# The last feed-forward block of an S4D layer with a ReLU network: its sums are turned back through five banks of PSUM instead of one

## The chip, the cores and the metric

The kernel runs on one core of one Trainium2 chip. The engines named here are TensorE (PE in the profile; PEld is its weight load), VectorE (DVE), ScalarE (ACT), GpSimd (POOL) and SyncE (SP). Matmul results go to PSUM, of which a core has eight banks of 128 x 512 fp32; VectorE and ScalarE read them from there. The metric is the time of one execution in microseconds, the median of several runs; less is better.

## What is computed

A block with adaptive layer norm: six vectors are made from a condition `c`, a normalised input goes through a long convolution (the S4D part, by Fourier transforms) and is added back, and the result goes through a feed-forward network with ReLU and is added back again. The second half is what the change is about:

```python
    h = _layernorm(x, axis=-1) * (1 + cb) + sb
    x = x + gb * _B_ref(h, B_w1, B_w2)
    ...
    def _B_ref(x, w1, w2):
        h = jnp.einsum("bsd,df->bsf", x, w1)
        zero = jnp.zeros_like(h)
        h = jnp.maximum(h, zero)
        return jnp.einsum("bsf,fd->bsd", h, w2)
```

There are 2048 tokens of 576 columns, and the hidden width is 4608. All values are fp32.

## The kernel before

The tokens are worked on in four blocks of 512 (`NB = 4`). The convolution of the first block is computed ahead; from then on the feed-forward network of block b runs on TensorE while the other engines prepare block b + 1.

**The feed-forward loop.** `ffn` (a generator, lines 1128 to 1276) goes over 4 x 36 steps, one for each 128 hidden columns of each block. A step makes 128 hidden columns for 512 tokens in one PSUM bank (tag `hps`, two banks, line 1179), ScalarE and VectorE take it out as a high and a low part (`hh`, `hl`, lines 1184 and 1185), and `second` multiplies both with the second weight and adds into five accumulators (`acc0` to `acc4`, five banks, line 1204). Each accumulator holds 128 of the 576 output columns, the last one the remaining 64 twice over (a high and a low part of the weights stacked), with the 512 tokens along the free dimension. With one more bank (tag `cps`, `nps = 1`) for transposes and all else, the eight banks are taken.

**The end of a block.** When the 36th step of a block has been added, `ffn` calls `evacuate` (line 1278): five ScalarE instructions (line 1283) copy the accumulators to SBUF, times the column's `gb`; the four full ones go to `oT` and the last to `o4`. `finish` (line 1289) then turns the result so that tokens lie on the partitions. For each of four groups of 128 tokens it makes four TensorE transposes into the `cps` bank (line 1301), adds the bank to the residual `x2` with VectorE (line 1304, 512 columns), makes one product with `ident2` (an identity stacked twice, which adds the two halves of the last accumulator) into the same bank (line 1307), adds that (line 1310, 64 columns), and stores 128 rows of 576 columns to DRAM from GpSimd's queue (line 1312). For blocks 0 to 2 `finish` is a generator whose pieces are worked in between the next block's matmuls; for block 3 nothing is left beside it, and `main` runs it through at the end (line 699).

**What sets the order.** Instructions are issued in the order of the code and wait for each other's results through semaphores that the framework puts in; each engine takes its own in order. A tile of a pool with one buffer can be written again only when its last reader is done. So with `nps = 1` the transposes of a token group wait until VectorE has read the `cps` bank.

Of the kernel before, what the change touches and what calls it, by code (L numbers as in the profile page):

```python
# [10 lines left out]
F32 = mybir.dt.float32  # L11
F32R = mybir.dt.float32r
I32 = mybir.dt.int32
AF = mybir.ActivationFunctionType
ALU = mybir.AluOpType
# [3 lines left out]
P = 128  # L19
L = 2048  # L20
D = 576
N = 128
F = 4608
NB = 4
NF = F // P
# [440 lines left out]
class Body:  # L466
# [187 lines left out]
    def main(self, ctx, kg, first, late):  # L654
        nc, tc, I = self.nc, self.tc, self.I
        sm = self.pool(ctx, "sm1")
        self.fcU, self.fcK, self.gc = (sm.tile([P, 4, 2, P], F32, name=n) for n in ("fcU", "fcK", "gc"))
        self.ended = -1
        self.gens = []
        self.start = self.ffn(self.gens)  # L660
        with ExitStack() as c:
            self.conv0(ctx, c, kg, first, late)
        self.nps = 1
        self.cps = self.pool(ctx, "cps", space=PSUM)
        self.fps = self.pool(ctx, "fps", space=PSUM)

        self.cvs = ExitStack()

        def pool(s):
            self.cv = self.pool(self.cvs, f"cv{s}")  # L670

        def block0():
            yield from kg.rest(
                self.cps,
                [(h + 6 * i, b) for h in range(6) for i, b in enumerate(((1, 2, 3), (1,)))],
            )
            self.xp.append(self.pool(ctx, "xb"))
            self.x2p.append(self.xp[1])
            pool(1)
            yield from self.conv(1)  # L680

        def block1():
            yield from self.finish(0)
            yield -1
            self.cvs.close()
            yield from kg.rest(self.cps, [(h, (2, 3)) for h in range(6, 12)])
            pool(2)
            yield from self.conv(2)

        def block2():  # L690
            yield from self.finish(1)
            yield from self.conv(3)

        self.gens += block0(), block1(), block2(), self.finish(2)
        with tc.issue_after(self.ends[0]), tc.issue_after(self.ends[1]):
            next(self.start)
        for _ in self.start:
            pass
        for _ in self.finish(3):
            pass  # L700
        self.cvs.close()

    def spec(self, name):
# [424 lines left out]
    def ffn(self, gens):  # L1128

        nc, I, ff = self.nc, self.I, self.ff  # L1130
        v = self.v
        n = NB * NF
# [3 lines left out]
        def load_r1(g):  # L1136
            r1[g] = ff.tile([P, 5, P], F32, tag="r1", bufs=2, name="r1")
            self.kept(nc.sync.dma_start(out=r1[g], in_=I["w1"][g % NF]))

        def load_r2(g):  # L1140
            r2[g] = ff.tile([P, D], F32, tag="r2", bufs=2, name="r2")
            self.kept(nc.sync.dma_start(out=r2[g], in_=I["w2"][(g % NF) * P : (g % NF) * P + P, :]))

        def low1(g):
            w = w1[g] = ff.tile([P, 2, 5, P], F32R, tag="w1", bufs=2, name="w1")
            if g >= NF:
                nc.sync.dma_start(
                    out=w[:, 1].rearrange("p k c -> p (k c)").bitcast(F32), in_=self.L1d[g % NF]
                )

        def split1(g):

            w, r = w1[g], r1.pop(g)
            nc.scalar.activation(w[:, 0], r, AF.Copy)  # L1154
            if g < NF:
                v(w[:, 1], r, w[:, 0], op=ALU.subtract)
                late.append((self.L1d[g], w[:, 1].rearrange("p k c -> p (k c)")))

        def split2(g):

            w = w2[g] = ff.tile([P, 1152], F32R, tag="w2", bufs=3, name="w2")
            r = r2.pop(g)
            nc.scalar.activation(w[:, 0:D], r, AF.Copy)  # L1163
            if g < NF:
                v(w[:, D:640], r[:, 512:D], w[:, 512:D], op=ALU.subtract)
                v(w[:, 640:], r[:, :512], w[:, :512], op=ALU.subtract)
                late.append((self.L2d[g], w[:, D:]))
            else:
                nc.sync.dma_start(out=w[:, D:].bitcast(F32), in_=self.L2d[g % NF])

        def first(g):
            xh, xl, xs = self.xT[g // NF]
            w = w1.pop(g)
            ps = self.fps.tile([P, 512], F32, tag="hps", bufs=2, name="hps")
            ops = [(w[:, 0, 4], xs), (w[:, 1, 4], xs)]
            for k in range(4):
                ops += [(w[:, 0, k], xh[:, k]), (w[:, 0, k], xl[:, k]), (w[:, 1, k], xh[:, k])]
            for i, (a, x) in enumerate(ops):
                nc.tensor.matmul(ps, a, x, start=(i == 0), stop=(i == 13))  # L1179
                if i == 6:  # L1180
                    step(g)
            hh = ff.tile([P, 512], F32R, tag="hh", bufs=3, name="hh")
            hl = ff.tile([P, 512], F32R, tag="hl", bufs=3, name="hl")
            nc.scalar.activation(hh, ps, AF.Relu)  # L1184
            nc.vector.scalar_tensor_tensor(hl, ps, 0.0, hh, op0=ALU.max, op1=ALU.subtract)  # L1185
            return hh, hl
# [27 lines left out]
        def step(g):  # L1214

            at[0] += 1
            at[1] = g
            target = self.rate(g // NF) * (at[0] % 144 or 144)
            gen = gens[g // NF]
            v = pe = 0.0  # L1220
            room = (9.0, 7.0, 7.0, 7.0)[g // NF] - sum(recent[-3:])
            recent.append(0.0)
            while done[0] < target and v < min(room, 2.7) and pe < 2:
                w = next(gen, 0)
                if gen.gi_frame is None or w == -1:
                    return
                if w is None:
                    pe += 1
                    done[0] += 0.7
                else:  # L1230
                    v += w
                    recent[-1] = v
                    done[0] += w
# [13 lines left out]
        for g in range(n + 2):  # L1247
            if g < n:
                if g + 2 < n:
                    load_r1(g + 2)  # L1250
                if g + 1 < n:
                    load_r2(g + 1)
                for dst, src in late:
                    nc.sync.dma_start(out=dst, in_=src.bitcast(F32))
                late.clear()
                if g:
                    split2(g)
                if g and g + 1 < n:
                    split1(g + 1)
                waiting.append((g, *first(g)))  # L1260
                if g + 2 < n:
                    low1(g + 2)
                step(g)
            if g > 1:
                e = waiting[0][0]
                second(*waiting.pop(0))
                if e % NF == NF - 1:
                    self.evacuate(e // NF)
            if g == 2:
                yield  # L1270
            if g < n:
                step(g)
                if g % NF == NF - 1:
                    for _ in gens[g // NF]:
                        pass
                    done[0] = 0.0

    def evacuate(self, b):
        o = self.spec("oT").rearrange("p a b c -> p (a b c)")[:, :2048]
        o = o.rearrange("p (i t) -> p i t", i=4)  # L1280
        o4 = self.cv.tile([P, 512], F32, tag="o4", bufs=1, name="o4")
        for i in range(5):
            self.nc.scalar.activation(
                o[:, i] if i < 4 else o4, self.acc[i], AF.Copy, scale=self.m["gb"][:, i : i + 1]
            )
        self.oT = (o, o4)
        self.ended = b

    def finish(self, b):

# [103 lines left out]
```

## Time and profile before

| what | before |
|---|---|
| median of 3 runs | 1411.89 us (1408.91 to 1412.83) |
| the profiled execution's own time | 1413.05 us |
| its span, first to last instruction | 1411.3 us |
| mean granted TensorE clock | 0.928 of full speed |
| last accumulating matmul of block 3 starts | 1396.33 us |
| last store issued | 1407.09 us |

The profile is of one execution. Its times are counted from the span's start, and 1.75 us of the execution's own time lie outside the span. Rows of the timeline name a line of the kernel; the line numbers are those of the code before, and after the change lines from 700 on are one less, from the new function on 33 more.

### The profile page before, as it was taken

Reading aid. Unit: us, or ns where it says so; the run is one execution under the profiler, and the core shown is the slowest. Engines: PE = TensorE matmul, PEld = TensorE weight load, DVE = VectorE, ACT = ScalarE, POOL = GpSimd, SP = SyncE. Lnnn points to the kernel's source line nnn. Section 1 sums busy time; section 2 is a strip of 40 time slices with the busy share of each in tenths; the row PEclk is TensorE's granted clock in tenths of the full one; section 3 lists DMA queues with packets and bytes.
Section 4 is the critical chain, followed back from the end, with each engine's and each line's share of the span. In section 5 each row is a group of like instructions: output and inputs, shape, how many; then the busy total and the mean of one; then the engine's idle time right before and its main releaser. Section 6 shows DMA issues by size and latency. Waiting matters only on the chain. (4 is left out here: it accounts for less than half of the span.)

```text
span 1411.3 us, 25953 instructions
## 1 busy us (share of the span) xinstructions
PE 1243.7 (88%) x10600; PEld 984.0 (70%) x10600; DVE 881.8 (62%) x1353; ACT 502.7 (36%) x1008; POOL 197.8 (14%) x271
## 2 busy tenths in 40 slices
PE   6023677999999988799999989999999999999997
PEld 3023455778777776577777867777887888888885
DVE  4987968999875796658744986263999232010111
ACT  6975224222223412432233224434322253233331
POOL 1776311011111100021011010000010000000000
PEclk9555688999999999899999999999999999999998
DMA  6665777689887947489678995665988657666661
GB/s 189 226 245 197 282 262 285 222 290 328 277 292 242 322 155 296 159 318 374 223 249 309 330 368 167 194 227 175 386 313 316 200 156 212 201 191 199 196 187 57
DMA packets 135510, 346.36 MB, mean 245 GB/s; under 512 B 23456, under 2 KB 23744, under 8 KB 135392
## 3 DMA queue, kind: packets, MB, share of 16 engines
q1 hardware_dynamic: 108112, 221.57, 48.2%
q0 software_dynamic: 26992, 122.55, 23.6%
q8 instruction: 83, 1.36, 0.4%
q10 hardware_dynamic: 288, 0.59, 0.1%
q14 instruction: 35, 0.29, 0.1%
HBM read 263.26 MB, written 81.40 MB: 244 GB/s over the span
## 5 line engine op out<-in xcount | busy, mean ns | idle before, releaser
L1204 PE MATMUL acc<-hh,w 128*128 128x512 f32 x1296 | 429.2, 404 | 6.0 <-DVE w L488 6.0
L1179 PE MATMUL hps<-xh,w 128*128 128x512 f32 x1152 | 398.1, 406 | 0.0
L1185 DVE SCALAR_TENSOR_TENSOR hl<-hps,hh 128x512 fp32r<-128x512 f32 x144 | 99.1, 688 | 323.6 <-ACT hh L1184 323.3
L1204 PEld LDWEIGHTS acc<-hh,w 128*128 128x128 f32 x1296 | 244.5, 190 | 59.8 <-DVE w L488 7.6
L1204 PE MATMUL acc<-hl,w 128*128 128x512 f32 x720 | 280.5, 399 | 0.0
L1179 PEld LDWEIGHTS hps<-xh,w 128*128 128x128 f32 x1152 | 219.3, 191 | 48.2 <-ACT xh L982 0.6
L1179 PE MATMUL hps<-xl,w 128*128 128x512 f32 x576 | 230.0, 399 | 0.2 <-DVE xl L987 0.2
L1184 ACT ACTIVATE hh<-hps 128x512 fp32r<-128x512 f32 x144 | 86.0, 598 | 338.8 <-PE hps L1179 336.1
L1163 ACT ACTIVATE w<-r 128x576 fp32r<-128x576 f32 x144 | 98.7, 686 | 259.6 <-PE acc L1204 217.3
L1204 PEld LDWEIGHTS acc<-hl,w 128*128 128x128 f32 x720 | 136.1, 189 | 28.5
L1179 PEld LDWEIGHTS hps<-xl,w 128*128 128x128 f32 x576 | 110.3, 191 | 24.8 <-DVE xl L987 1.3
L246 PE MATMUL kps<-W,W 128*32 128x16 f32 x2304 | 39.8, 219 | 92.9 <-POOL W L59 60.0
L1154 ACT ACTIVATE w<-r 128x640 fp32r<-128x640 f32 x144 | 105.5, 733 | 38.5 <-DMA L1d<-w 33.5
L1179 PE MATMUL hps<-xs,w 128*128 128x512 f32 x288 | 103.6, 421 | 11.0 <-ACT w L1154 4.4
L246 PEld LDWEIGHTS kps<-W,W 128*32 128x32 f32 x2304 | 37.6, 151 | 96.0 <-POOL W L59 61.4
L421 PEld LDWEIGHTS kps<-W1r,W2r 128*32 128x32 f32 x3456 | 68.5, 146 | 31.1 <-issue 21.7
L488 DVE TENSOR_TENSOR Y<-Y,T 128x1152 f32<-128x1152 f32 x64 | 85.0, 1351 | 0.2
L421 PE MATMUL kps<-W1r,W2r 128*32 128x48 f32 (+2 forms) x3456 | 77.2, 238 | 7.8 <-issue 4.9
L1312 POOL DMA_DIRECT2D out_dram<-x x16 | 8.8, 550 | 492.4 <-DVE x L1310 492.4
L1179 PEld LDWEIGHTS hps<-xs,w 128*128 128x128 f32 x288 | 54.2, 192 | 24.9 <-DVE w L488 5.3
L488 DVE TENSOR_TENSOR w<-r,w 128x64 fp32r<-128x64 f32 (+2 forms) x108 | 58.3, 572 | 14.3 <-ACT w L1154 12.0
L725 ACT ACTIVATE Z<-ps_f 128x288 f32<-128x288 f32 x104 | 42.2, 409 | 68.6 <-PE ps_f L724 62.5
(192 smaller groups left out, 1414.6 us busy)
## 6 DMA issues: line engine op xcount, KB each, us to landing
r<-in_w_dram SPq DMA_DIRECT2D x144, 320.0 KB, 3.7
r<-in_w_dram SPq DMA_DIRECT2D x144, 288.0 KB, 3.5
w<-L1d SPq DMA_DIRECT2D x108, 320.0 KB, 3.0
w<-L2d SPq DMA_DIRECT2D x108, 288.0 KB, 3.2
W2r<-W2d POOLq DMA_DIRECT2D x18, 1536.0 KB, 10.0
W2d<-W SPq DMA_DIRECT2D x12, 1536.0 KB, 7.7
Ua<-Ud POOLq DMA_DIRECT2D x15, 1152.0 KB, 10.7
W<-W1d POOLq DMA_DIRECT2D x18, 768.0 KB, 10.0
```

What stands on the lines that cost most here:

```text
L246: self.nc.tensor.matmul(ps[32 * dd : 32 * dd + 32, 12 * u + q, :], W2[:, r, :, ch], W1[:, u, :, r, ch], start=(r == 0), stop=(r == 1),)
L421: nc.tensor.matmul(ps[32 * dd : 32 * dd + 32, q, :], W2[:, r, :, ch], W1[:, :na, r, ch], start=(r == 0), stop=(r == 1),)
L488: return self.kept(self.nc.vector.tensor_tensor(*args, **kw))
L725: nc.scalar.activation(Z[:, n2, c], ps[:, :PC], AF.Copy)
L1154: nc.scalar.activation(w[:, 0], r, AF.Copy)
L1163: nc.scalar.activation(w[:, 0:D], r, AF.Copy)
L1179: nc.tensor.matmul(ps, a, x, start=(i == 0), stop=(i == 13))
L1184: nc.scalar.activation(hh, ps, AF.Relu)
L1185: nc.vector.scalar_tensor_tensor(hl, ps, 0.0, hh, op0=ALU.max, op1=ALU.subtract)
L1204: nc.tensor.matmul(acc[i], a, x, start=(f == 0 and j in (0, 3, 6, 9, 12)), stop=(f == NF - 1 and j in (2, 5, 8, 11, 13)),)
L1312: nc.gpsimd.dma_start(out=ov[:, n2], in_=x2[:, n2])
```

## The change

Block 3 no longer goes through `evacuate` and `finish(3)`, but through a new method, `last_block`, that `main` calls at the same place. Since the last hidden column has been multiplied by then, the two `hps` banks are free, and each accumulator's bank is free once it has been copied.

- The copies to SBUF alternate: ScalarE does accumulators 0, 2 and 4, VectorE 1 and 3.
- The transposes go accumulator by accumulator, each into the matching quarter of four banks: one bank for each token group, the two of `hps`, the `cps` bank and the bank of `acc0`.
- The four products for the last 64 columns go to a fifth bank, that of `acc1`, and one VectorE instruction adds them for all four token groups.
- The stores are issued from SyncE's queue.

```diff
@@
-        for _ in self.finish(3):
-            pass
+        self.last_block()
         self.cvs.close()
@@
-                if e % NF == NF - 1:
+                if e % NF == NF - 1 and e < n - 1:
                     self.evacuate(e // NF)
@@
+    def last_block(self):
+
+        nc, m = self.nc, self.m["gb"]
+        x2 = self.x2.pop(NB - 1)
+        ov = self.out[L - 512 :, :].rearrange("(m n) d -> m n d", n=4)
+        o = self.spec("oT").rearrange("p a b c -> p (a b c)")[:, :2048]
+        o = o.rearrange("p (i t) -> p i t", i=4)
+        o4 = self.cv.tile([P, 512], F32, tag="o4", bufs=1, name="o4")
+        tok = [slice(n2 * P, (n2 + 1) * P) for n2 in range(4)]
+        ps = []
+        for i in range(5):
+            t = o[:, i] if i < 4 else o4
+            if i % 2:
+                nc.vector.tensor_scalar(t, self.acc[i], m[:, i : i + 1], None, op0=ALU.mult)
+            else:
+                nc.scalar.activation(t, self.acc[i], AF.Copy, scale=m[:, i : i + 1])
+            if i == 0:
+                for tag, bufs in (("hps", 2), ("hps", 2), ("acc0", 1)):
+                    ps.append(self.fps.tile([P, 4, P], F32, tag=tag, bufs=bufs, name="ps_l"))
+                ps.insert(2, self.cps.tile([P, 4, P], F32, tag="cps", bufs=self.nps, name="ps_l"))
+            if i < 4:
+                for n2 in range(4):
+                    nc.tensor.transpose(ps[n2][:, i], o[:, i, tok[n2]], self.ident)
+        ps4 = self.fps.tile([P, 4, 64], F32, tag="acc1", name="ps_l4")
+        for n2 in range(4):
+            nc.tensor.matmul(ps4[:, n2], o4[:, tok[n2]], self.ident2, start=True, stop=True)
+        for n2 in range(4):
+            xo = x2[:, n2, 0:512]
+            nc.vector.tensor_tensor(xo, ps[n2].rearrange("p a b -> p (a b)"), xo, op=ALU.add)
+            if n2 == 0:
+                xo = x2[:, :, 512:D]
+                nc.vector.tensor_tensor(xo, ps4, xo, op=ALU.add)
+            nc.sync.dma_start(out=ov[:, n2], in_=x2[:, n2])
```

VectorE at the end of the program, before: `hl` is the low part of a hidden step, `x_3` the residual of block 3, `ps_o` the one bank with the transposes or with the last columns.

```order
L1185 SCALAR_TENSOR_TENSOR hl<-hps,hh 128x512 x31
L1304 TENSOR_TENSOR x_3_9308<-ps_o,x_3_9308 128x512
L1310 TENSOR_TENSOR x_3_9308<-ps_o_12827,x_3_9308 128x64
L1304 TENSOR_TENSOR x_3_9308<-ps_o,x_3_9308 128x512
L1310 TENSOR_TENSOR x_3_9308<-ps_o_12837,x_3_9308 128x64
L1304 TENSOR_TENSOR x_3_9308<-ps_o,x_3_9308 128x512
L1310 TENSOR_TENSOR x_3_9308<-ps_o_12847,x_3_9308 128x64
L1304 TENSOR_TENSOR x_3_9308<-ps_o,x_3_9308 128x512
L1310 TENSOR_TENSOR x_3_9308<-ps_o_12857,x_3_9308 128x64
```

The same engine and place after the change; `acc` are the accumulators' banks, `ps_l` the five banks, `oT` the copy.

```order
L1184 SCALAR_TENSOR_TENSOR hl<-hps,hh 128x512 x31
L1301 TENSOR_SCALAR oT<-acc_108_11338,m_gb 128x512
L1301 TENSOR_SCALAR oT<-acc_108_11340,m_gb 128x512
L1316 TENSOR_TENSOR x_3_9308<-ps_l,x_3_9308 128x512 x2
L1319 TENSOR_TENSOR x_3_9308<-ps_l_12841,x_3_9308 128x4x64
L1316 TENSOR_TENSOR x_3_9308<-ps_l,x_3_9308 128x512 x2
```

Two copies have come in ahead of the adds, and the four narrow adds have become one, which stands third among the adds and not second as in the code.

TensorE at the same place, before:

```order
L1204 MATMUL acc_108_11341<-hh,w_12750 128x512
L1204 MATMUL acc_108_11341<-hl,w_12750 128x512
L1301 MATMUL ps_o<-ident,oT 128x128 x4
L1307 MATMUL ps_o_12827<-ident_199,o_12815 128x64
L1301 MATMUL ps_o<-ident,oT 128x128 x4
L1307 MATMUL ps_o_12837<-ident_199,o_12815 128x64
L1301 MATMUL ps_o<-ident,oT 128x128 x4
L1307 MATMUL ps_o_12847<-ident_199,o_12815 128x64
L1301 MATMUL ps_o<-ident,oT 128x128 x4
L1307 MATMUL ps_o_12857<-ident_199,o_12815 128x64
```

And after:

```order
L1203 MATMUL acc_108_11340<-hh,w_12750 128x512 x2
L1203 MATMUL acc_108_11340<-hl,w_12750 128x512
L1203 MATMUL acc_108_11341<-hh,w_12750 128x512
L1203 MATMUL acc_108_11341<-hl,w_12750 128x512
L1310 MATMUL ps_l<-ident,oT 128x128 x16
L1313 MATMUL ps_l_12841<-ident_199,o_12815 128x64 x4
```

The sixteen transposes and the four products, which stood in four turns of four and one, are two runs of sixteen and four. The four stores have left GpSimd's queue and stand at the end of SyncE's, behind the last weight loads. Ahead of these places the rows of every engine are the same in both kernels.

## The prediction

> **What bounds the kernel now.** The page comes first: its top two rows say how much room there is in general.
>
> ```profile
> span 1411.3 us, 25953 instructions
> PE 1243.7 (88%) x10600; PEld 984.0 (70%) x10600; DVE 881.8 (62%) x1353; ACT 502.7 (36%) x1008; POOL 197.8 (14%) x271
> ```
>
> TensorE is busy for 88% of the span, and nothing in the change touches its long part. The change concerns the stretch behind the last accumulating matmul, so I read next the timeline of the end. Columns: start, duration, engine, line, operation, count, and in brackets the idle time before it with what ended it.
>
> ```profile
> 1394.27 2.73 ACT L1283 ACTIVATE oT<-acc,m_gb 128x512 f32<-128x512 f32 x4 [6.43 <-PE acc L1204]
> 1395.88 0.39 PE L1204 MATMUL acc<-hl,w 128*128 128x512 f32 x1
> ...
> 1396.33 0.39 PE L1204 MATMUL acc<-hl,w 128*128 128x512 f32 x1
> 1396.57 0.81 PE L1301 MATMUL ps_o<-ident,oT 128*128 128x128 f32 x4
> 1396.89 0.68 ACT L1283 ACTIVATE o<-acc,m_gb 128x512 f32<-128x512 f32 x1
> 1397.41 0.69 DVE L1304 TENSOR_TENSOR x<-ps_o,x 128x512 f32<-128x512 f32 x1 [8.85 <-PE ps_o L1301]
> 1398.25 0.41 PE L1307 MATMUL ps_o<-ident,o 128*128 128x64 f32 x2 [0.88 <-DVE x L1304]
> 1398.70 0.22 DVE L1310 TENSOR_TENSOR x<-ps_o,x 128x64 f32<-128x64 f32 x1 [0.59 <-PE ps_o L1307]
> 1398.97 0.66 PE L1301 MATMUL ps_o<-ident,oT 128*128 128x128 f32 x4 [0.32 <-DVE x L1310]
> ...
> 1403.95 1.11 PE L1301 MATMUL ps_o<-ident,oT 128*128 128x128 f32 x4 [0.32 <-DVE x L1310]
> 1406.57 0.22 DVE L1310 TENSOR_TENSOR x<-ps_o,x 128x64 f32<-128x64 f32 x1 [0.78 <-PE ps_o L1307]
> 1407.09 0.54 POOL L1312 DMA_DIRECT2D out_dram<-x  x1 [2.36 <-DVE x L1310]
> ```
>
> The last accumulating matmul ends at 1396.33 + 0.39 = 1396.72. From there to the span's end are 14.6 us. The reader should see a relay: TensorE fills the one bank, VectorE empties it, and only then may TensorE go on. The table of waits for this stretch (us, times, longest) confirms it:
>
> ```profile
> DVE x L1304 <- PE ps_o L1301: 11.9, 4, 8.9
> PE ps_o L1307 <- DVE x L1304: 3.2, 4, 0.9
> DVE x L1310 <- PE ps_o L1307: 2.7, 4, 0.8
> ```
>
> Each engine waits for the other in turn. Of the first row's 11.9 us, 8.9 is VectorE having nothing to do while the matmuls ran. The stretch in five pieces shows what stands behind the relay (clock and DMA are the last three columns):
>
> ```profile
> 1396.70:1401.10 4.40, 2.17 (x13) 1.27 (x11) 1.82 (x4) 0.87 (x2) 0.54 (x1) 1.00 0.17 67
> 1401.10:1407.10 6.00, 3.48 (x12) 2.31 (x12) 1.84 (x5) 0.00 (x0) 1.09 (x3) 0.52 0.26 98
> 1407.10:1408.10 1.00, 0.00 (x0) 0.00 (x0) 0.00 (x0) 0.00 (x0) 0.54 (x1) 0.50 0.00 0
> 1408.10:1409.10 1.00, 0.00 (x0) 0.00 (x0) 0.00 (x0) 0.00 (x0) 0.00 (x0) 0.50 0.77 295
> 1409.10:1411.30 2.20, 0.00 (x0) 0.00 (x0) 0.00 (x0) 0.00 (x0) 0.00 (x0) 0.50 0.00 0
> ```
>
> The granted clock falls from 1.00 to about half near 1401.3, in the middle of the relay. After the last store is issued at 1407.09 come 1.0 us without data, 1.0 us of data and 2.2 us in which nothing moves. So the relay lasts 10.4 us (1396.7 to 1407.1) and the store with what follows it 4.2 us.
>
> **The change, part by part.** Two durations are needed first: the step from one transpose to the next, and the adds.
>
> ```profile
> 1398.97 0.33 PE L1301 MATMUL ps_o<-ident,oT 128*128 128x128 f32 x1 [0.32 <-DVE x L1310]
> 1403.95 0.47 PE L1301 MATMUL ps_o<-ident,oT 128*128 128x128 f32 x1 [0.32 <-DVE x L1310]
> 1398.25 0.29 PE L1307 MATMUL ps_o<-ident,o 128*128 128x64 f32 x1 [0.88 <-DVE x L1304]
> L1304 DVE TENSOR_TENSOR x<-ps_o,x 128x512 f32<-128x512 f32 x4 | 2.8, 692 | 11.9 <-PE ps_o L1301 11.9
> L1310 DVE TENSOR_TENSOR x<-ps_o,x 128x64 f32<-128x64 f32 x4 | 0.9, 224 | 2.7 <-PE ps_o L1307 2.7
> L978 DVE TENSOR_SCALAR xf<-ps_t,m_cb,m_sb 128x512 f32<-128x512 f32 x2 | 1.6, 810 | 2.3 <-PE ps_t L973 2.1
> ```
>
> At full clock four transposes take 0.66 and the first alone 0.33, so each further one adds 0.11; at half clock (1.11 - 0.47) / 3 = 0.21. One last-column product is two records in the trace, 0.41 together and 0.29 for the first, so 0.12 a record.
>
> *Copies.* ScalarE keeps sums 0, 2 and 4, VectorE takes 1 and 3. Sum 3 is complete at 1395.88 + 0.39 = 1396.27, in the before as in the after. No row shows VectorE's multiply from PSUM by one column; the nearest are the add, 0.69, and line 978's two-constant form, 0.81. I take 0.81 and get 1397.1. Nothing is queued behind it on VectorE but the adds. ScalarE can read sum 4 from about 1396.8. The copies are hidden as long as TensorE asks for sum 3 later than 1397.1, and it asks at about 1397.9 (below). Worth: nothing; without that cover a late copy would cost at most its own 0.8.
>
> *Transposes.* 16 now run in a row, sum by sum into four banks, with no waiting for VectorE. The thirteenth, the first of sum 3, starts at 1396.57 + 12 x 0.11 = 1397.9, and completes bank 0 at 1398.2. The sixteenth starts at 1398.2; the eight records of the last columns follow, the last starting at 1398.3 + 7 x 0.12 = 1399.2 and ending near 1399.5.
>
> *Adds.* VectorE's order has two wide adds, the one for the last columns of all rows, then two wide adds. Two wide ones: 1398.25 + 2 x 0.69 = 1399.6, behind which the last columns are ready by 0.1 us. The new add has 256 elements a partition; the trace has 64 (0.22) and 512 (0.69), and four separate ones would be 0.90. On the line between them it is 0.22 + 192/448 x 0.47 = 0.43, to 1400.06. Two more: 1401.44. Before, the last add ended at 1406.57 + 0.22 = 1406.79. So the relay shrinks by 5.35 us: that is the gross gain, and it is the bank waits and the second half at half clock that go.
>
> *Stores.* The four stores move from GpSimd's queue to SyncE's. SyncE has no load left to issue by then, and nothing is queued behind the wait of the first store on VectorE but the other three. They used to leave one in each turn of the relay, so that each had the DMA engines to itself. Now the first waits for the third add, leaves near 1400.16 with the second right behind, and the fourth leaves near 1401.54 (0.1 for the hand-over; the timeline shows 0.05 from VectorE to TensorE and 0.30 from VectorE to GpSimd). What a store of this size costs on each queue, when little else runs:
>
> ```profile
> L1312 POOL DMA_DIRECT2D out_dram<-x x1: 543/543/543, 1407.1 to 1407.1; - x1
> DMA to landing us min/median/max: 2.4/2.4/2.4
> ...
> L358 SPq DMA_DIRECT2D kd<-ke x2: 482/539/596, 182.9 to 183.4; - x2
> DMA to landing us min/median/max: 2.4/2.5/2.6
> 182.80:184.00 1.20, 1.20 (x4) 0.82 (x3) 1.20 (x2) 0.05 (x1) 0.00 (x0) 0.50 0.05 19
> 184.00:185.60 1.60, 1.60 (x5) 0.86 (x3) 1.53 (x3) 0.00 (x0) 0.00 (x0) 0.50 0.92 369
> ```
>
> The second pair is two stores of the same 288 KB from SyncE's queue, early in the kernel. Alone, a store lands 2.4 us after its issue on either queue. The pair was issued 0.5 apart (182.9, 183.4), and the second landed 0.72 behind the first (183.4 + 2.6 against 182.88 + 2.4): the transfers queue on DMA engines that are 92% busy. Four queued stores land at 1400.16 + 2.4 + 3 x 0.72 = 1404.72; the fourth alone would land at 1401.54 + 2.4 = 1403.94. The queue is last, and takes back 0.8 us. From the last landing (1407.09 + 2.4 = 1409.49) to the span's end the before needs 1.81; I see no reason for a change there, since the same landing has to be seen by the same closing barrier. End: 1406.53, so 4.8 us less.
>
> The Trainium skill, page "DMA: Bandwidth & Descriptors", section "Specifications", gives about 0.6 us to the first byte from SyncE's queue and about 1 us from GpSimd's; by that the sum would be about 5.2. The rows don't bear it out for stores: 1.1 us without data on SyncE's (182.88 to 184.0), 1.0 on GpSimd's (1407.09 to 1408.10). I leave that gain out.
>
> **The rivals.** *No queueing:* the fourth store lands by its own 2.4, at 1403.94, and the end is 1405.75: 5.55 us less, 1406.3. For it: a lone store shows 295 KB in under 1 us. Against it: the pair.
>
> *Stores from SyncE land later:* these rows are its stores while the convolution ran beside them.
>
> ```profile
> L1254 SPq DMA_DIRECT2D L2d<-w x36: 319/432/1621, 229.6 to 587.8; - x36
> DMA to landing us min/median/max: 3.5/4.8/16.1
> ```
>
> With the median 4.8 the end is 1401.54 + 4.8 + 1.81 = 1408.15: 3.15 less, 1408.7. Against it: at the end nothing else uses the DMA engines.
>
> *TensorE falls to half clock at once,* as it did in the before some 4.5 us behind the last accumulating matmul. With 0.21 and 0.24 a step the last columns end near 1402.0 instead of 1399.5 and the third add near 1402.5, so the stores leave 2.4 later: 2.4 less, 1409.5. Against it: the clock was 1.00 to 1401.1 with idle gaps between the transposes, and the new work ends by 1399.5. The Trainium skill, page "TensorE: Matmul & The Clock Gate", section "Part 4: PE-mode transpose", says that transposes do not count as a busy TensorE for the clock; if so, this case is the way it would show. The trace neither refutes that nor needs it.
>
> *Slower:* a store at the very end lands as the slowest of those 36, 16.1 us after issue. Then the end is 1401.54 + 16.1 + 1.81 = 1419.45, 8.15 later than now: 1420.0. It decides from a landing of 1411.3 - 1.81 - 1401.54 = 7.95 us on. The maximum belongs to a queue with loads and large convolution transfers in it; here there are four stores and nothing more.
>
> **How the numbers follow.** The profiled execution took 1413.05 us with a span of 1411.3; the median of the three runs is 1411.89, 1.2 below it. 1413.05 - 4.8 = 1408.25 in its frame, 1411.89 - 4.8 = 1407.1 in the median's, which I give. A measurement of this kernel can tell about 0.3%, 4.2 us, from no change; the forecast is only 0.6 beyond, and the runs of the before lie 3.9 apart (1408.91 to 1412.83), a median of three being good to about 1 us. So even if the mechanism is right it reads as faster about 7 times in 10.
>
> Chances: forecast 0.62, no queueing 0.14, later landing 0.11, half clock 0.10, slower 0.03. Faster by over 0.3%: 0.62 x 0.72 + 0.14 x 0.85 + 0.11 x 0.2 = 0.59, say 0.6; slower 0.03; the rest, 0.37, within. The range reaches from no queueing less the spread of the runs, 1404.0, to the half clock, 1409.8.
>
> **What would show it.** Right: transposes 0.11 apart with clock 1.00, VectorE busy without a gap from about 1398.25 to 1401.4, stores landing 0.7 apart, 1.8 us behind the last. Wrong: a gap ahead of the new add (TensorE late), the new add far from 0.43, the last landing more than 3.5 us behind its issue, or a stretch ahead of 1394 that differs by more than 1 us.

## The result, and the profile after

The changed kernel takes 1402.89 us (median of 20 runs, 1396.08 to 1409.36), the kernel before 1408.93 us in the same series (median of 20 runs, 1402.57 to 1419.48). The ratio is 0.9948, 95% interval 0.9933 to 0.9964: 5.1 to 9.4 us less. Faster was the likeliest case of the prediction, but its time was 4.2 us too high and its range, which began at 1404.0, missed the result.

The profiled execution of the changed kernel has a span of 1401.2 us (before 1411.3) at a mean granted clock of 0.931 (0.928). Its timeline at the end, with columns as in the prediction:

```profile
1391.38 0.69 ACT L1303 ACTIVATE oT<-acc,m_gb 128x512 f32<-128x512 f32 x1 [0.67 <-PE acc L1203]
1392.06 0.75 DVE L1301 TENSOR_SCALAR oT<-acc,m_gb 128x512 f32<-128x512 f32 x1 [0.61 <-PE acc L1203]
1392.09 0.39 PE L1203 MATMUL acc<-hl,w 128*128 128x512 f32 x1
...
1392.32 1.91 PE L1310 MATMUL ps_l<-ident,oT 128*128 128x128 f32 x16
1392.52 0.69 ACT L1303 ACTIVATE o<-acc,m_gb 128x512 f32<-128x512 f32 x1 [0.45 <-PE acc L1203]
1393.94 1.29 DVE L1316 TENSOR_TENSOR x<-ps_l,x 128x512 f32<-128x512 f32 x2 [1.12 <-PE ps_l L1310]
...
1394.06 1.00 PE L1313 MATMUL ps_l<-ident,o 128*128 128x64 f32 x8
1395.14 0.41 DVE L1319 TENSOR_TENSOR x<-ps_l,x 128x256 f32<-128x256 f32 x1
1395.47 1.28 DVE L1316 TENSOR_TENSOR x<-ps_l,x 128x512 f32<-128x512 f32 x2
1395.58 1.87 SPq L1320 DMA_DIRECT2D out_dram<-x  x4
```

The relay is gone: 16 transposes in a row, 8 records of products in a row, five additions without a gap. In the table of waits (us, times, longest) the wide adds of VectorE wait for TensorE only once, for 1.1 us, where before the four of them waited 11.9 us in all. No wait of TensorE for VectorE is left:

```profile
DVE x L1316 <- PE ps_l L1310: 1.1, 1, 1.1
ACT oT L1303 <- PE acc L1203: 0.7, 1, 0.7
DVE oT L1301 <- PE acc L1203: 0.6, 1, 0.6
ACT o L1303 <- PE acc L1203: 0.4, 1, 0.4
```

The stretch in pieces (busy time of PE, PEld, DVE, ACT and POOL; clock; DMA share; GB/s) shows what is last now. The second and third row look closer at the moment of the first byte:

```profile
1392.50:1396.30 3.80, 2.57 (x24) 2.43 (x22) 2.68 (x6) 0.69 (x1) 0.00 (x0) 1.00 0.00 0
1396.05:1396.35 0.30, 0.00 (x0) 0.00 (x0) 0.30 (x2) 0.00 (x0) 0.00 (x0) 1.00 0.00 0
1396.35:1396.65 0.30, 0.00 (x0) 0.00 (x0) 0.30 (x1) 0.00 (x0) 0.00 (x0) 1.00 0.79 292
1396.30:1399.60 3.30, 0.00 (x0) 0.00 (x0) 0.45 (x1) 0.00 (x0) 0.00 (x0) 1.00 0.95 358
1399.60:1401.20 1.60, 0.00 (x0) 0.00 (x0) 0.00 (x0) 0.00 (x0) 0.00 (x0) 0.53 0.00 0
```

For 3.3 us the DMA engines are 95% busy while nothing else runs but the last addition: the four stores queue. Then come 1.6 us without data. The stores themselves (duration of an issue in ns, first and last start), with the time from issue to landing:

```profile
L1320 SPq DMA_DIRECT2D out_dram<-x x4: 338/413/466, 1395.6 to 1397.0; - x4
...
DMA to landing us min/median/max: 2.1/2.6/3.0
```

The first lands 2.1 us after its issue, the fourth 3.0 us after its own, at 1396.98 + 3.0 = 1399.98.

To compare executions I count from the end of the last accumulating matmul; what lies behind it I call the tail, what lies ahead the head.

| us from the end of the last accumulating matmul | before | predicted | after |
|---|---|---|---|
| that matmul's end, in the span | 1396.72 | 1396.72 | 1392.48 |
| first wide add starts | 0.69 | 1.53 | 1.46 |
| first store issued | 2.49 | 3.44 | 3.10 |
| last store issued | 10.37 | 4.82 | 4.50 |
| last landing | 12.77 | 8.00 | 7.50 |
| end of the span: the tail | 14.58 | 9.81 | 8.72 |

The two spans differ by 10.1 us: 5.86 in the tail, and 4.24 in the head, where both kernels issue the same instructions.

### The profile page after: what moved, and what is told of

Read it like the earlier page. It is cut to its first block, busy times and chain, and to the rows that moved or that the text cites. A ratio compares the mean times of both kernels' runs of the same rounds, so it can differ in the third digit from the quotient of the medians.

```text
span 1401.2 us, 25949 instructions
## 1 busy us (share of the span) xinstructions
PE 1233.9 (88%) x10600; PEld 978.8 (70%) x10600; DVE 878.3 (63%) x1352; ACT 501.7 (36%) x1006; POOL 196.0 (14%) x267
## 5 line engine op out<-in xcount | busy, mean ns | idle before, releaser
L931 PE MATMUL ps_i<-V,gc 128*128 128x288 f32 x136 | 43.2, 450 | 13.5 <-DVE x L488 10.1
## 6 DMA issues: line engine op xcount, KB each, us to landing
W2r<-W2d POOLq DMA_DIRECT2D x18, 1536.0 KB, 10.1
```

The lines of the kernel that those rows point to most:

```text
L931: self.nc.tensor.matmul(ps[:, :PC], a, b, start=(i == 0), stop=(i == len(todo) - 1))
```

## The experiments

Three questions: whether the 4.24 us of the head belong to the change, what sets the tail now, and which parts of the change earn the 5.86. Single executions of one kernel differ by several us, so the tail is read from each trace; a median is given where many runs were made. In the expectations theory A is that the change acts on the tail alone and that the first store with the queue behind it sets the tail's end; other letters are rivals, each with what it expects.

| kernel | end of last accumulating matmul | first store | last store | last landing | tail |
|---|---|---|---|---|---|
| before, once more | 1395.15 | 2.49 | 10.66 | 13.06 | 14.85 |
| after, once more | 1392.21 | 3.10 | 4.50 | 7.5 | 8.69 |
| before, last stores from SyncE | 1393.12 | 2.23 | 10.49 | 12.6 | 13.78 |
| after, stores from GpSimd | 1387.98 | 3.37 | 4.96 | 8.4 | 10.12 |
| after, one bank | 1394.35 | 2.38 | 5.96 | 8.1 | 9.25 |
| after, copies on ScalarE | 1390.88 | 3.11 | 4.51 | 7.5 | 8.72 |
| after, stores from two queues | 1389.74 | 3.11 | 4.30 | 7.5 | 8.76 |
| after, group by group | 1396.75 | 1.61 | 3.80 | 6.0 | 7.15 |
| after, sum 3 row by row | 1392.16 | 2.31 | 4.50 | 6.7 | 7.94 |
| after, narrow adds | 1390.39 | 2.91 | 4.50 | 7.3 | 8.51 |
| after, one store | 1393.74 | 4.30 | 4.30 | 8.5 | 9.36 |

The second column is a time in the span, the others count from it.

### Both kernels once more

No edit: the kernel before is timed against itself, and the changed one again.

> The kernel before, unchanged, timed against itself. Theory A: ratio 1.000, tail 14.6 within 0.2, and the end of the last accumulating matmul differs from the 1396.72 of the first profile by some us, as much as it did between before and after. Theory B: the last accumulating matmul ends at 1396.7 within 1 us, so that the 4.24 us of the first two profiles would be the work of the change.

> The changed kernel once more. The tail is the time from the end of the last accumulating matmul to the end of the span: 14.58 us in the profile of before, 8.72 in that of after, 5.86 less; the two profiles also differ by 4.24 us ahead of the tail. Theory A, only the tail is changed and the stretch ahead varies from execution to execution: tail 8.7 within 0.2, ratio to before about 0.9958 (5.9 of 1409), and the last accumulating matmul ends anywhere between 1385 and 1400. Theory B, the change also shortens the stretch ahead by some 4 us: ratio about 0.993, and the last accumulating matmul ends near 1392.5 again.

Before against itself: ratio 0.9999 (0.9976 to 1.0022), medians 1410.6 and 1409.36. The changed kernel: 1403.53 against 1409.36, ratio 0.9953 (0.9933 to 0.9974). The tails came out as 14.85 and 8.69 us, 6.2 apart, and the medians 5.8 apart here and 6.0 in the first series. So what the medians show is about the tail. Two points need a word. The tail of before is a little over the 14.6 within 0.2 of theory A, because the clock fell earlier in this relay (last section). And the last accumulating matmul of the changed kernel ended at 1392.21, as theory B had it; that of before ended at 1395.15, against B, and the spread of the other executions in the table shows that the first was chance.

The head varies by itself. These rows show the copy of sum 3, which stands beside the last accumulating matmul, in the earliest and in the latest of the eleven executions above; first the kernel with its stores on GpSimd's queue:

```profile
1387.56 0.75 DVE L1301 TENSOR_SCALAR oT<-acc,m_gb 128x512 f32<-128x512 f32 x1 [0.61 <-PE acc L1203]
```

Then the kernel that goes group by group:

```profile
1396.33 0.75 DVE L1301 TENSOR_SCALAR oT<-acc,m_gb 128x512 f32<-128x512 f32 x1 [0.61 <-PE acc L1203]
```

The same copy starts at 1387.56 in the one and at 1396.33 in the other, 8.8 us later, on the same chip and with identical instructions ahead of it. The 4.24 us between the two first profiles lie well within that. The spread arises ahead of block 3's feed-forward network: from its first accumulating matmul to its last it takes 220.3 to 220.4 us in all thirteen traces, before and after. It goes together with the granted clock: of the 20 timed runs of the changed kernel the four shortest (1396.08 to 1397.76) have a mean clock of 0.937 or 0.938, the two longest (1407.93 and 1409.36) 0.928 and 0.929. What sets that clock was not tried. What this does not settle: the three heads of the old tail have a mean of 1395.0, the ten of new tails 1392.1, and with such a spread a true difference of a microsecond or two in the head can be neither shown nor excluded.

### The queue of the stores, in both kernels

After the change, back to GpSimd's queue:

```diff
-            nc.sync.dma_start(out=ov[:, n2], in_=x2[:, n2])
+            nc.gpsimd.dma_start(out=ov[:, n2], in_=x2[:, n2])
```

> The changed kernel with the four stores back on GpSimd's queue. Theory A, the move to SyncE's queue brings a hand-over of 0.03 instead of 0.30, a first byte 0.75 instead of 1.0 behind the issue and a shorter close: tail 9.8 (1.1 more), with 1.8 us from the last landing to the end of the span. Rival D, the shorter close of after comes from something else: tail 9.2, with 1.2 us behind the last landing.

The kernel before, with block 3's stores alone on SyncE's queue:

```diff
-            nc.gpsimd.dma_start(out=ov[:, n2], in_=x2[:, n2])
+            (nc.sync if b == NB - 1 else nc.gpsimd).dma_start(out=ov[:, n2], in_=x2[:, n2])
```

> The kernel before with one edit: the last block's four stores are issued from SyncE's queue. The relay of one bank stays. Theory A, the queue alone is worth its hand-over, its earlier first byte and its shorter close: tail 13.4 instead of 14.6. Rival D, the queue is worth nothing by itself: tail 14.3 to 14.6.

With GpSimd's queue the tail is 10.12 us, 1.4 more, where theory A expected 1.1. The timeline and the pieces of this kernel:

```profile
1390.64 0.41 DVE L1319 TENSOR_TENSOR x<-ps_l,x 128x256 f32<-128x256 f32 x1
1390.97 1.28 DVE L1316 TENSOR_TENSOR x<-ps_l,x 128x512 f32<-128x512 f32 x2
1391.35 2.13 POOL L1320 DMA_DIRECT2D out_dram<-x  x4 [205.47 <-DVE x L1319]
```

```profile
1392.10:1392.40 0.30, 0.00 (x0) 0.00 (x0) 0.15 (x1) 0.00 (x0) 0.30 (x1) 1.00 0.00 0
1392.40:1392.70 0.30, 0.00 (x0) 0.00 (x0) 0.00 (x0) 0.00 (x0) 0.30 (x2) 1.00 0.92 353
...
DMA to landing us min/median/max: 2.4/2.9/3.4
```

Four things cost. The issue starts 0.30 behind the third add's end (1390.64 + 0.41 = 1391.05), where SyncE's starts 0.03 behind it (1395.55 to 1395.58). The first byte comes 1.05 behind the issue (1391.35 to 1392.40), where SyncE's comes 0.77 behind (1395.58 to 1396.35). And the close, from the last landing (1392.94 + 3.4 = 1396.3) to the end of the span at 1398.1, is 1.8 us instead of 1.2. Together these make 1.15. The rest is that the landings take longer to follow each other: from the first (1391.35 + 2.4) to the last they take 2.6 us instead of 2.3.

The kernel before with SyncE's queue shows the same without any other edit. Its last turn and its stores:

```profile
1395.35 8.60 SPq L1312 DMA_DIRECT2D out_dram<-x  x4
...
1402.63 0.69 PE L1307 MATMUL ps_o<-ident,o 128*128 128x64 f32 x2 [0.78 <-DVE x L1304]
1403.36 0.23 DVE L1310 TENSOR_TENSOR x<-ps_o,x 128x64 f32<-128x64 f32 x1 [0.78 <-PE ps_o L1307]
```

```profile
L1312 SPq DMA_DIRECT2D out_dram<-x x4: 332/334/338, 1395.3 to 1403.6; - x4
...
DMA to landing us min/median/max: 2.1/2.1/2.1
```

The last store leaves at 1403.6, lands 2.1 later instead of 2.4, and the span ends 1.2 behind that, at 1406.9. From the last add's end (1403.59) to the end of the span are 3.3 us; in the first profile of before they were 4.5 (1406.79 to 1411.3). So behind the last add the queue alone is worth 1.2 us here, and 1.4 in the changed kernel, where the stores also queue. The tail shrank by only 0.8, and not to the 13.4 that theory A expected, since in this execution the clock had halved earlier in the relay: the products of the second turn took 0.69, where the first profile has 0.43, and the last add ended 10.5 us behind the last matmul instead of 10.1.

### One bank instead of four

The transposes go group by group through the `cps` bank; copies, the products' bank, the common narrow add and SyncE's queue stay.

```diff
...
         for n2 in range(4):
-            nc.tensor.matmul(ps4[:, n2], o4[:, tok[n2]], self.ident2, start=True, stop=True)
-        for n2 in range(4):
+            t = self.cps.tile([P, 4, P], F32, tag="cps", bufs=self.nps, name="ps_l")
+            for i in range(4):
+                nc.tensor.transpose(t[:, i], o[:, i, tok[n2]], self.ident)
+            if n2 == 0:
+                for n3 in range(4):
+                    nc.tensor.matmul(ps4[:, n3], o4[:, tok[n3]], self.ident2, start=True, stop=True)
             xo = x2[:, n2, 0:512]
-            nc.vector.tensor_tensor(xo, ps[n2].rearrange("p a b -> p (a b)"), xo, op=ALU.add)
+            nc.vector.tensor_tensor(xo, t.rearrange("p a b -> p (a b)"), xo, op=ALU.add)
```

> The changed kernel with all transposes through one bank again, token group by token group; copies shared, one narrow add from a bank of its own, stores from SyncE's queue as in the change. Theory A, the waits for the bank are only part of the relay, the rest was the narrow product and add in the same bank and the half clock: last add ends 5.9 us behind the last accumulating matmul (4.3 in the changed kernel), tail 9.2. Rival E, the four further banks are the gain: tail 12 or more.

The tail is 9.25 us, only 0.5 more than with four banks. Its last two turns:

```profile
1396.73 3.92 SPq L1317 DMA_DIRECT2D out_dram<-x  x4
...
1398.16 0.69 DVE L1313 TENSOR_TENSOR x<-ps_l,x 128x512 f32<-128x512 f32 x1 [0.75 <-PE ps_l L1308]
...
1398.91 0.66 PE L1308 MATMUL ps_l<-ident,oT 128*128 128x128 f32 x4 [0.79 <-DVE x L1313]
1399.60 0.69 DVE L1313 TENSOR_TENSOR x<-ps_l,x 128x512 f32<-128x512 f32 x1 [0.75 <-PE ps_l L1308]
```

The relay is back, 1.44 us a turn at full clock, yet the last add ends only 5.94 behind the last matmul (1400.29 less 1394.35) against 4.27 with four banks: of those 1.67 us the stores give 1.1 back, because they leave 0.7, 1.4 and 1.4 us apart and no longer queue, each landing 2.1 behind its issue. The relay of before cost more by its second hand-over in each turn, for the 64 columns that went through the same bank, and by the half clock that it ran into. In the first profile of before the third turn starts here:

```profile
1401.17 0.99 PE L1301 MATMUL ps_o<-ident,oT 128*128 128x128 f32 x4 [0.32 <-DVE x L1310]
```

From the second turn's start (1398.97, in the prediction's rows) that is 2.20 us at full clock, 0.76 more than the 1.44 here, and a turn at half clock took 2.9. No run takes away one of these two alone. Taken back alone, the queue costs 1.4 of the tail's 5.86 us, the one bank for the transposes 0.5 and the copies (next) nothing; the rest, about 3.9, is put down to the second hand-over and the half clock by subtraction.

### Copies on ScalarE alone

No copy is left to VectorE:

```diff
-            if i % 2:
+            if i > 4:
```

> The changed kernel with ScalarE making all five copies, as before. Theory A, the copies lie behind the accumulating matmuls and the first transposes: tail 8.7 within 0.1. Rival F, sharing the copies is part of the gain: tail 9.0 or more, with TensorE waiting for the fourth copy.

The tail is 8.72 us, the same as the changed kernel's. Sum 4 is copied from 1391.05 to 1391.73, long ahead of the last columns at 1392.46:

```profile
1390.72 1.91 PE L1310 MATMUL ps_l<-ident,oT 128*128 128x128 f32 x16
1391.05 0.68 ACT L1303 ACTIVATE o<-acc,m_gb 128x512 f32<-128x512 f32 x1
1392.34 1.29 DVE L1316 TENSOR_TENSOR x<-ps_l,x 128x512 f32<-128x512 f32 x2 [9.62 <-PE ps_l L1310]
1392.46 1.00 PE L1313 MATMUL ps_l<-ident,o 128*128 128x64 f32 x8
```

The copies are hidden, as the prediction had them; sharing them is worth nothing here.

### Stores from two queues

```diff
-            nc.sync.dma_start(out=ov[:, n2], in_=x2[:, n2])
+            (nc.scalar if n2 % 2 else nc.sync).dma_start(out=ov[:, n2], in_=x2[:, n2])
```

> The changed kernel with stores 1 and 3 issued from ScalarE's queue and 0 and 2 from SyncE's. Theory A, the stores queue on the DMA engines, whichever queue they come from: last landing 7.5 us behind the last accumulating matmul, tail 8.7 within 0.2. Rival G, they queue within one issue queue: last landing near 6.4, tail 7.6.

The stores leave a little earlier and land no earlier; the tail is 8.76 us. The data stretch of this kernel:

```profile
1392.80:1393.60 0.80, 0.00 (x0) 0.00 (x0) 0.80 (x3) 0.00 (x0) 0.00 (x0) 1.00 0.00 0
1393.60:1396.80 3.20, 0.00 (x0) 0.00 (x0) 0.41 (x1) 0.00 (x0) 0.00 (x0) 0.73 0.98 368
1396.80:1398.50 1.70, 0.00 (x0) 0.00 (x0) 0.00 (x0) 0.00 (x0) 0.00 (x0) 0.50 0.01 1
```

98% and 368 GB/s against 95% and 358: the queue is in the DMA engines, not in the issuing engine.

### When the first store goes out

If the stores' transfers are last, only the moment counts at which the first of them starts. Four kernels move that moment or the number of stores. Group by group: the four transposes of a token group follow each other, the product of group n comes behind the transposes of group n + 1, in a bank of its own, and each row has its own narrow add.

```diff
...
+        def last(n2):
+            nc.tensor.matmul(ps4[n2], o4[:, tok[n2]], self.ident2, start=True, stop=True)
+
         for n2 in range(4):
-            nc.tensor.matmul(ps4[:, n2], o4[:, tok[n2]], self.ident2, start=True, stop=True)
+            for i in range(4):
+                nc.tensor.transpose(ps[n2][:, i], o[:, i, tok[n2]], self.ident)
+            if n2:
+                last(n2 - 1)
+        last(3)
...
```

> The five banks, but the transposes token group by token group, with the last columns of a group in a bank of their own right behind, four narrow adds, and a store behind each. Theory A, the four stores queue on the DMA engines from the first issue on, so what counts is how early the first leaves: first store 1.6 us behind the last accumulating matmul instead of 3.1, last landing bound by VectorE near 6.1 instead of 7.5, tail 7.3, ratio to before about 0.995. Rival C, TensorE and VectorE set the end: the same work with three more VectorE instructions gives a tail of 8.7 to 9.1.

Sums 0 to 2 as in the changed kernel, then sum 3 and the last columns row by row:

```diff
-            if i < 4:
+            if i < 3:
...
         for n2 in range(4):
-            nc.tensor.matmul(ps4[:, n2], o4[:, tok[n2]], self.ident2, start=True, stop=True)
+            nc.tensor.transpose(ps[n2][:, 3], o[:, 3, tok[n2]], self.ident)
+            nc.tensor.matmul(ps4[n2], o4[:, tok[n2]], self.ident2, start=True, stop=True)
...
```

> Sums 0, 1 and 2 are transposed as before the edit, then sum 3 and the last columns row by row (one transposition and one product for row 0, then for row 1, and so on, each product into a bank of its own), and each row has its own wide and narrow addition and store. Everything else is the changed kernel's. The tail is counted from the end of the last accumulating matmul to the end of the span (8.7 us in the changed kernel). Theory A, that the tail is the first store's issue plus four queued stores (5.6 us from the first issue to the span's end) and that nothing else of the last additions counts: the first store's issue comes 2.3 to 2.5 us behind the last matmul instead of 3.1, and the tail is 8.0 to 8.2 us. Rival R, that the last addition sets the end: there are eight additions of 0.33 to 0.61 us start to start instead of five, so the last ends about 0.2 to 0.4 us later than the 4.3 us of the changed kernel, and the tail is 8.9 to 9.1 us.

Only the common narrow add taken apart:

```diff
-            if n2 == 0:
-                xo = x2[:, :, 512:D]
-                nc.vector.tensor_tensor(xo, ps4, xo, op=ALU.add)
+            xo = x2[:, n2, 512:D]
+            nc.vector.tensor_tensor(xo, ps4[:, n2], xo, op=ALU.add)
```

> The changed kernel with a 64-column addition of its own for each row in place of the one 256-column addition. The tail of the changed kernel is 8.7 us. Theory A (only the first store's issue counts): the first row's narrow addition still waits for the products, which end 2.6 us behind the last matmul, and is about 0.1 to 0.2 us shorter than the 0.41 of the common one; the first store goes out 2.9 to 3.0 us behind the last matmul and the tail is 8.5 to 8.6 us. Rival R (the last addition counts): three more additions of about 0.2 to 0.3 us move the last addition's end by 0.5 to 0.7 us, and the tail is 9.0 to 9.4 us.

And one store for all four rows:

```diff
-            nc.sync.dma_start(out=ov[:, n2], in_=x2[:, n2])
+        nc.sync.dma_start(out=ov, in_=x2)
```

> The changed kernel with one store of all four rows behind the last addition in place of four stores. The tail of the changed kernel is 8.7 us. Theory A, that the four stores run at the DMA engines' rate one behind the other (1.15 MB at 375 to 400 GB/s): the issue moves from 3.1 to about 4.3 us behind the last matmul, the landing comes 4.3 to 4.5 us later, the close is 1.2 us, and the tail is 9.8 to 10.0 us. Rival S, that the spacing of 0.7 to 0.8 us is the price of each store as a transfer of its own and not of its bytes: one store lands about 2.1 to 2.7 us behind its issue, and the tail is 7.6 to 8.2 us.

From the first store's issue to the span's end are 5.62 us in the changed kernel, 5.54 group by group (1398.36 to 1403.9), 5.63 row by row (1394.47 to 1400.1), 5.60 with narrow adds (1393.30 to 1398.9). The first store itself moved from 3.10 to 1.61, 2.31 and 2.91, and the tail followed: 7.15, 7.94, 8.51 (expected 7.3, 8.0 to 8.2, 8.5 to 8.6). Here is the best of them, group by group:

```profile
1396.59 1.21 PE L1315 MATMUL ps_l<-ident,oT 128*128 128x128 f32 x8
...
1397.51 0.69 DVE L1321 TENSOR_TENSOR x<-ps_l,x 128x512 f32<-128x512 f32 x1 [0.42 <-PE ps_l L1315]
...
1398.11 0.21 DVE L1323 TENSOR_TENSOR x<-ps_l,x 128x64 f32<-128x64 f32 x1
...
1398.36 2.52 SPq L1324 DMA_DIRECT2D out_dram<-x  x4
...
1399.70 0.68 DVE L1321 TENSOR_TENSOR x<-ps_l,x 128x512 f32<-128x512 f32 x1
1400.30 0.21 DVE L1323 TENSOR_TENSOR x<-ps_l,x 128x64 f32<-128x64 f32 x1
```

The rows are 0.73 apart (1398.97, 1399.70), about the 0.7 to 0.8 by which queued stores land apart, and each store lands 2.1 to 2.2 behind its issue: VectorE feeds the DMA engines without a queue. The rival that the last addition sets the end would have had the row-by-row kernel at 8.9 to 9.1 and the narrow adds at 9.0 to 9.4, since in both the last add ends later than in the changed kernel (4.46 and 4.47 us behind the last matmul, against 4.27); both came out shorter.

One store for all rows, with its trace's pieces:

```profile
1398.00:1398.90 0.90, 0.00 (x0) 0.00 (x0) 0.01 (x1) 0.00 (x0) 0.00 (x0) 0.90 0.15 61
1398.90:1402.20 3.30, 0.00 (x0) 0.00 (x0) 0.00 (x0) 0.00 (x0) 0.00 (x0) 0.50 0.82 341
1402.20:1403.10 0.90, 0.00 (x0) 0.00 (x0) 0.00 (x0) 0.00 (x0) 0.00 (x0) 0.50 0.00 0
```

It lands 4.2 us after its issue at 1398.04. The rival that 0.7 to 0.8 is the price of a store and not of its bytes (2.1 to 2.7) falls. The tail is 9.36 and not theory A's 9.8 to 10.0: it landed 0.1 to 0.3 sooner, and the close took 0.9 us instead of 1.2, which neither theory had (last section).

Group by group was timed in full: 1402.41 us, ratio 0.9956 (0.993 to 0.9983) to the kernel before. Its tail is 1.6 us shorter than the changed kernel's, 0.1% of the time, and the medians cannot show that.

## Why the prediction was wrong

**Right: the mechanism.** The relay went, the copies and the transposes are hidden, the clock held at 1.00 past the last addition, the stores became a queue on the DMA engines. All four rivals fell: the queue is there (358 GB/s, landings 0.7 to 0.8 apart, no gain from two queues), stores from SyncE's queue landed after 2.1 to 3.0 us and not 4.8 or 16.1, and TensorE had done by 2.6 us behind the last matmul (1394.06 + 1.00 less 1392.48), 4.6 us ahead of the fall of its clock at 1399.7. In the ten traces of changed kernels TensorE was always done before the clock fell, by 1.2 us at the least.

**Mis-sized, 1.1 us: the tail.** The prediction had 4.77 of gain, the traces show 5.86. *"Two wide ones: 1398.25 + 2 x 0.69"*: consecutive adds overlap. From the start of the first wide add to that of the add for the last columns are 1.20 us (1393.94 to 1395.14), not 1.38, and that add lasts 0.41, not 0.43. With a hand-over of 0.03 instead of 0.1 and a start 0.07 earlier, the first store is 0.34 earlier. *"Alone, a store lands 2.4 us after its issue on either queue"*: it is 2.1 on SyncE's here. From the first issue to the last landing are 4.40 us (3.10 to 7.50), 2.1 and three steps of 0.7 to 0.8, and not 2.4 + 3 x 0.72 = 4.56: 0.16. The pair from which 2.4 was taken was issued early in the kernel, with TensorE busy throughout at half clock; why it took longer there was not tried. *"I see no reason for a change there"*: the close is 1.2 us behind SyncE's stores and 1.8 behind GpSimd's, in both kernels: 0.59. Together 1.09. Most of this is the queue's: the prediction gave the move to SyncE's queue 0.2 for the hand-over and nothing else, and it is worth 1.4 when taken back alone.

The dismissed rule belongs here. The Trainium skill, page "DMA: Bandwidth & Descriptors", section "Specifications", gives about 0.6 us to the first byte on SyncE's queue and about 1 us on GpSimd's. The runs show 0.77 and 1.05: smaller on SyncE's queue as the page has it, by 0.28 and not by 0.4. The prediction set it aside for the 1.1 us of that early pair.

**The step that failed, 3 us: the frame.** *"1411.89 - 4.8 = 1407.1 in the median's, which I give"* and *"a median of three being good to about 1 us"*. The median of 20 runs of the same kernel is 1408.93, 2.96 lower, and that of 28 others 1409.36. Three runs that lay within 3.9 us said nothing of a spread of 17 (1402.57 to 1419.48). 1408.93 - 4.8 would have been 1404.1, and with the tail's measured 5.86 it is 1403.1, 0.2 from what was measured. The miss of 4.2 is so 3.0 for the base, 1.1 for the tail and 0.1 to 0.2 for what remains. The range took in the unknown prices of the tail, but ended below at the spread of three runs. Lowered by 3 us for the base's own uncertainty, its low end would have been 1401.0 and held the result. The base is not all of it: the 4.8 us of gain lie just below the 5.1 to 9.4 of these 20 runs of each kernel (the second series, 3.7 to 9.4, would allow them). The upper end, 1409.8, was called the half clock's, whose own sum gives 1409.5.

**The head.** The prediction named "a stretch ahead of 1394 that differs by more than 1 us" as a sign that it is wrong. It differed by 4.24, and the sign was a bad one: the head moves by 8.8 us between executions with the same instructions ahead of the tail.

## What to carry to other kernels

Count a change at the end of a kernel from the last instruction that both versions share, and judge the total against the spread of many runs: here the base of three runs was a larger error than all the tail's unknown prices. When the stores at the end queue, the tail is the first store's issue plus their bytes, so order the last work to finish the first piece early, and not to finish all pieces together. Issue the last stores from a queue with a short hand-over and close: SyncE's was worth 1.2 to 1.4 us in these kernels.

## What the runs showed of the hardware

- The end of the program comes 1.8 us behind the last landing from GpSimd's queue and about 1.2 us behind SyncE's, but 0.9 us behind a single store of all rows. The traces show why. The close is an exchange of all engines through semaphores, in which GpSimd has to answer SyncE. With the stores on GpSimd's queue, a DRAIN on GpSimd starts right behind the last store, at 1392.8, and ends 4.5 us later, 1.0 us behind the last landing; GpSimd answers only then. In the changed kernel it began at 1189.8 and was long over, and GpSimd answers 0.5 us behind the landing. With the single store SyncE passes one semaphore wait behind the landing instead of six, which are 0.06 us apart, and GpSimd answers 0.2 us behind it.
- VectorE adds of 512 columns last 0.68 to 0.69 us each and start 0.60 to 0.61 apart when nothing holds them.
- The clock's fall to half is not fixed to the work. In the first profile of before it came 4.6 us behind the last accumulating matmul, in the third turn's transposes (0.99, where full clock has 0.66 and half 1.11); in that of the kernel before once more it came 3.8 us behind, in the second turn's products (0.60, where full clock has 0.41 and half 0.69). In the changed kernel it came 7.2 us behind (1399.7 less 1392.48), with one store for all rows, which has the same work on TensorE, 5.0 us behind (0.90 of full in the piece from 1398.00 to 1398.90). In each of the thirteen traces all changes of the clock, from the first to the last, lie on one grid of 3.41 us, to within 2 ns; where that grid lies against the end of the program differs from execution to execution.

The two closes, with stores on GpSimd's queue and in the changed kernel (shortest, median and longest in ns, first and last start; the longest is the first):

```profile
L1423 POOLq DRAIN  x3: 46/108/4522, 1392.8 to 1397.8; - x3
...
L1423 POOLq DRAIN  x3: 46/99/5525, 1189.8 to 1400.9; - x3
```

The rows of the kernel before once more, second and third turn:

```profile
1398.84 0.60 PE L1307 MATMUL ps_o<-ident,o 128*128 128x64 f32 x2 [0.78 <-DVE x L1304]
...
1399.76 1.11 PE L1301 MATMUL ps_o<-ident,oT 128*128 128x128 f32 x4 [0.32 <-DVE x L1310]
```

The Trainium skill, page "TensorE: Matmul & The Clock Gate", section "Part 4: PE-mode transpose", says that transposes don't count as a busy TensorE in the way that other matmuls do; no run here was made to separate that, and in none of the changed kernels did TensorE still work when the clock fell.
